# First down phase: where the weight blocks with index 5 and 6 are loaded and when, and chunk 2's output transposes 0.6 later

## The chip, the core and the metric

The kernel runs on one core of one Trainium2 chip. The metric is the device time of one execution in microseconds (us). A core has a matrix engine (PE, with its weight loads shown apart as PEld), a vector engine (DVE), a scalar engine (ACT), a general engine (POOL) and a sequencer for transfers (SP). Transfers between the chip's memory and the on-chip memory are asked for on the queues of SP, POOL and ACT; a queue works through its instructions in their order, so one that waits holds up those behind it.

## The reference

One transformer layer with adaptive layer norm: S = 2048 tokens, width D = 576, 32 heads of 18, a sliding window of 8 keys at distances 0, 2, ..., 14, and a gated feed-forward part of width 4608, without a nonlinearity.

```python
mod = (_silu(c) @ w_mod).reshape(c.shape[0], 6, 1, -1)
sa, ca, ga, sb, cb, gb = ...
h = _layernorm(x) * (1 + ca) + sa
x = x + ga * _A_ref(h, A_wqkv, A_wo)          # windowed attention, then @ wo
h = _layernorm(x) * (1 + cb) + sb
x = x + gb * _B_ref(h, B_w_gate, B_w_up, B_w_down)

def _B_ref(x, w_gate, w_up, w_down):
    h = (x @ w_gate) * (x @ w_up)
    return h @ w_down
```

## The kernel before

The 2048 tokens are cut into 8 chunks of 256. After a prologue (chunk 0's attention and the first steps of chunks 1 and 2) the chunks go through the feed-forward part in five groups, `GROUPS = [[0], [1, 2], [3, 4], [5, 6], [7]]`. For each group there is a gate-up phase (`gate_up`), in which PE makes the 36 tiles `hh[:, f]` of gate times up, and then a down phase (`down`, for the last group `down_last`), in which PE multiplies them by `w_down` into the sums `acc` (columns 0 to 511, line 895) and `accr` (columns 512 to 575, line 900). The attention of later chunks is slipped between these matmuls.

**The down phase of group 0.** One chunk of 256 tokens, so two blocks of 128 rows (`j`); for each of 36 steps `f` there is a pair `mm_a`, `mm_r` for each `j`. Four steps use one block of `w_down` (`FB = 4`, 128 x 4 x 576 bf16, 576 KB), so the phase has 9 blocks, index 0 to 8, and a group's blocks are numbered on from there: 9, 10 and 11 are blocks 0 to 2 of group 1. Steps 0 to 31 run in the loop; block 8 (steps 32 to 35) comes at the end, first all `accr` products, then all `acc` products. Then DVE scales the sums and adds the residual (lines 921 to 930), and the gate-up phase of group 1 follows on PE.

**Where the blocks lie.** `load_wd(g)` (line 171) asks for a block on POOL's queue. It goes to a place of its own if `wd_home` names one, and else to the next of three rotating buffers `wd`. For group 0, blocks 0, 1 and 2 go to the three buffers and blocks 3 and 4 to the half of the `hh` tile that a group of one chunk leaves free; all five are asked for during the gate-up phase. Before the change, block 5 is asked for at the end of block 0, 6 after 1, 7 after 2, then 8 after 5, 9 after 6 and 10 after 7, and 11 at the end of the phase: each goes into the buffer that was just read. `prod_t` holds four products of queries and shifted keys (128 x 1280 bf16 each, line 446) during the attention; groups 1, 2 and 3 already keep two of their blocks in it during their down phases (`ld_prods`, blocks 3 and 4 of the group, asked for at step 32 of the gate-up).

**What lies between the matmuls.** `first_down` lists pieces of later chunks' work in threads. A piece is (PE time, DVE time, marks it needs, its mark, wait until the mark counts, call). `timed` steps through the phase with these estimates, and places a piece behind the step at which its marks are reached, so the order of the instructions is fixed when the kernel is built. In this phase the pieces are: chunk 1's output product and residual (`b_w(1, j)`: lines 588 to 594), its layer norm (`b_ln`, `b_norm`), its transposes by transfer on SP's queue (`b_td`, line 620) and its modulation in place (`b_mod`: lines 294 and 296 on `h2T`); chunk 4's query, key and value products (`a_q`, `a_v`: lines 401, 424, 426), whose values are stored to `vd` on POOL's queue (line 431); and of chunk 2 the weighting of the gathered values (`b_mul`, `b_add`: lines 499 to 509, on the tiles `vsh` that line 440 loads on POOL's queue), then `b_o(2)`, which transposes the attention output `o_sb` on PE (line 517) and copies it to `oT` on ACT (lines 518, 519), then `b_w(2, j)` and its layer norm.

POOL's instructions around the phase are, in order: the loads of `vsh` for chunk 2, a memset of part of `hT` (line 386), the two stores of chunk 4's values, the loads of blocks 5, 6 and 7, then 8, 9, 10 and 11, and the loads of `vsh` for chunk 3.

Of the kernel before, what the change touches and what calls it, by code (L numbers as in the profile page):

```python
# [36 lines left out]
FB = 4  # L37
# [7 lines left out]
def kernel(  # L45
# [45 lines left out]
    def ps(shape, dt, name):  # L91
        return psp.tile(shape, dt, name=name, tag="bank")

    def js(j):
        return slice(j * P, (j + 1) * P)
# [48 lines left out]
    NBLK = FT // FB  # L144

    def load_wgu(g):
        if g >= NG * NBLK:
            return
        cs = slice((g % NBLK) * NB, (g % NBLK + 1) * NB)
        wb = wgu_home.pop(g, None)  # L150
        if wb is None:
            wb = wgup.tile([P, KF, 2, NB], BF, name="wgu")
        for t, wsrc in enumerate((B_w_gate, B_w_up)):
            r = nc.sync.dma_start(wb[:, :, t, :], wsrc[0:KF * P, cs].rearrange("(k p) n -> p k n", p=P))
        wgu_blk[g] = wb
        wgu_in[g] = r
# [6 lines left out]
    def load_wd(g):  # L163
        if g >= NG * NBLK:
            return
        r0 = (g % NBLK) * FB * P
        wb = wd_home.pop(g, None)
        if wb is None:
            wb = wdp.tile([P, FB, D], BF, name="wd")
        wd_blk[g] = wb  # L170
        return nc.gpsimd.dma_start(wb[:], B_w_down[r0:r0 + FB * P, :].rearrange("(k p) n -> p k n", p=P))  # L171
# [239 lines left out]
    def a_q(i, g):  # L411
        qk_tiles(i, QGRP[g], slice(0, CH), nc.scalar.copy)
        if g == 2:
            a_halo(i)
# [4 lines left out]
    def a_v(i, j):  # L419
        hT = aa[i]["hT"]  # L420
        pv = ps([P, VA * DH], F32, "pv")
        pvr = ps([P, VR * DH], F32, "pvr")
        for kt in range(KT):
            nc.tensor.matmul(pv[:], lhsT=hT[:, kt, js(j)], rhs=wv[:, kt, 0:VA * DH], start=(kt == 0), stop=(kt == KT - 1))  # L424
        for kt in range(KT):
            nc.tensor.matmul(pvr[:], lhsT=hT[:, kt, js(j)], rhs=wv[:, kt, VA * DH:D], start=(kt == 0), stop=(kt == KT - 1))
        v_sb = vstage.tile([P, DH, H], BF, name="v_sb")
        nc.scalar.copy(v_sb[:, :, 0:VA], pv[:].rearrange("p (h d) -> p d h", d=DH))
        nc.scalar.copy(v_sb[:, :, VA:H], pvr[:].rearrange("p (h d) -> p d h", d=DH))
        r0 = HALO + i * CH + j * P  # L430
        nc.gpsimd.dma_start(vd[r0:r0 + P, :], v_sb[:].rearrange("p d h -> p (d h)"))
        aa[i].setdefault("v", []).append(v_sb)
# [78 lines left out]
    def b_o(i):  # L511
        pA = ps([P, 4, CH], BF, "oT_pA")
        pB = ps([P, 1, CH], BF, "oT_pB")
        for m in range(KT):
            d = pA[:, m, :] if m < 4 else pB[:, 0, :]
            for j in range(ST):
                nc.tensor.transpose(d[:, js(j)], o_sb[:, j, m * P:(m + 1) * P], ident[:])
        nc.scalar.copy(oT[:, 0:4, :], pA[:])
        nc.scalar.copy(oT[:, 4, :], pB[:, 0, :])
# [64 lines left out]
    def b_w(i, j):  # L584
        pw = ps([P, 512], F32, "pw")
        pwr = ps([P, 64], F32, "pwr")
        for m in range(KT):
            nc.tensor.matmul(pwr[:], lhsT=oT[:, m, js(j)], rhs=wo[:, m, 512:D], start=(m == 0), stop=(m == KT - 1))
        for m in range(KT):
            nc.tensor.matmul(pw[:], lhsT=oT[:, m, js(j)], rhs=wo[:, m, 0:512], start=(m == 0), stop=(m == KT - 1))  # L590
        xt = x1p.tile([P, D], BF, name="x1")
        nc.vector.tensor_tensor(xt[:, 512:D], pwr[:], ga_bc[:, 512:D], ALU.mult)
        nc.vector.tensor_tensor(xt[:, 0:512], pw[:], ga_bc[:, 0:512], ALU.mult)
        nc.vector.tensor_tensor(xt[:], xt[:], x_res[i][:, j, :], ALU.add)
        x1.setdefault(i, []).append(xt)

    def b_ln(i):
        x_res.pop(i)
        bb[i]["xn"], bb[i]["rsq"], bb[i]["norm"] = layernorm(lambda j: x1[i][j], "b", i == 1)
# [238 lines left out]
    def among(n, step, threads):  # L838
        at, (seq, late) = [[] for _ in range(n)], timed([("f", f, step, 0.0, "") for f in range(n)], [], threads, step)
        for kind, x in seq:  # L840
            if kind == "f":
                f = x
            else:
                at[f].append(x)
        return at, late
# [39 lines left out]
    def down(gi, hh, bg):  # L885
        grp = GROUPS[gi]
        nj = ST * len(grp)
        last = FT - FB
        at, late = among(last, 0.25 * nj, bg)
        acc = [ps([P, 512], F32, "acc") for _ in range(nj)]  # L890
        accr = ps([P, 2 * ST, 64], F32, "accr")

        def mm_a(f, j):
            wb = wd_blk[gi * NBLK + f // FB]
            nc.tensor.matmul(acc[j][:], lhsT=hh[:, f, js(j)], rhs=wb[:, f % FB, 0:512],  # L895
                             start=(f == 0), stop=(f == FT - 1))

        def mm_r(f, j):
            wb = wd_blk[gi * NBLK + f // FB]
            nc.tensor.matmul(accr[:, j, :], lhsT=hh[:, f, js(j)], rhs=wb[:, f % FB, 512:D],  # L900
                             start=(f == 0 and j == 0), stop=(f == FT - 1), skip_group_check=True)

        for f in range(last):
            for j in range(nj):
                mm_a(f, j)
                mm_r(f, j)
            if f % FB == FB - 1:
                if f // FB not in (3, 4):
                    load_wd(gi * NBLK + f // FB + (5 if f < 3 * FB else 3))
            asks = (1, 5 * FB, 6 * FB + 2) if gi == 0 else (1, 4 * FB - 1, 6 * FB + 1)  # L910
            if f in asks:
                load_wgu((gi + 1) * NBLK + asks.index(f))
            for piece in at[f]:
                piece()
        xs = [t for i in grp for t in x1.pop(i)]
        for j in range(nj):
            for f in range(last, FT):
                mm_r(f, j)
        o_ts = [outp.tile([P, D], BF, name="o_t") for _ in range(nj)]
        t_r = outr.tile([P, 2 * ST, 64], BF, name="t_r")  # L920
        nc.vector.tensor_tensor(t_r[:, 0:nj, :], accr[:, 0:nj, :],
                                gb_bc[:, None, 512:D].to_broadcast([P, nj, 64]), ALU.mult)
        for j in range(nj):
            for f in range(last, FT):
                mm_a(f, j)
            nc.vector.tensor_tensor(o_ts[j][:, 0:512], acc[j][:], gb_bc[:, 0:512], ALU.mult)
        for j in range(nj):
            r0 = (grp[0] * ST + j) * P
            nc.vector.tensor_tensor(o_ts[j][:, 0:512], o_ts[j][:, 0:512], xs[j][:, 0:512], ALU.add)
            nc.vector.tensor_tensor(o_ts[j][:, 512:D], t_r[:, j, :], xs[j][:, 512:D], ALU.add)  # L930
            nc.sync.dma_start(out_flat[r0:r0 + P, :], o_ts[j][:])
        load_wd(gi * NBLK + NBLK + 2)
        return late
# [260 lines left out]

    def ld_prods(gi):
        for k in range(2):
            g = gi * NBLK + 3 + k
            wd_home[g] = prod_t[:, k * FB * D:(k + 1) * FB * D].rearrange("p (k d) -> p k d", d=D)
            load_wd(g)

# [33 lines left out]
    def first_down(late):  # L1234
        def q(g):
            return (0.53 if g == 2 else 1.07, 0, "h4", "-", 0, lambda: a_q(4, g))

        def v(j):
            return (1.2, 0, "h4", "-", 0, lambda: a_v(4, j))

        def out_1(first):
            return [(0, 0, "", "o1", 1.0, nop), (1.2, 1.35, "o1", "-", 0, lambda: b_w(1, 0)), (1.2, 1.35, "", "x1", 0.5, lambda: b_w(1, 1)),
                    (0, 2.5, "", "s1", 0.7, lambda: b_ln(1)), (0, 0, "s1", "n1", 2.3, lambda: b_norm(1)), (0, 0, "n1", "t1", 9.5, lambda: b_td(1)),
                    (0, 1.0, "t1", "-", 0, lambda: (b_mod(1, (3, 4), False), b_mod(1, (0, 1, 2), True)))]
        a4 = [(0, 0, "", "h4", 1.5, nop)]
        o2 = [(0.55, 0, "o21", "O2", 0.9, lambda: b_o(2)), (1.2, 1.35, "O2", "-", 0, lambda: b_w(2, 0)), (1.2, 1.35, "", "x2", 0.2, lambda: b_w(2, 1)),
              (0, 2.2, "", "s2", 0.7, lambda: b_ln(2)), (0, 1.5, "s2", "n2", 0.2, lambda: b_norm(2)), (0.55, 1.0, "n2", "-", 0, lambda: b_t(2))]
        return [a4, out_1(True), late + [(0, 0, "", "a2", 0.0, nop)] + values_of(2) + o2, [q(0), q(1), q(2), q(3), q(4), v(0), v(1)]]

# [61 lines left out]
```

## Time and profile before

| what | value |
|---|---|
| runs (median of 3; lowest, highest) | 552.38 us; 551.4, 554.15 |
| profiled execution: its own time, span | 551.74 us, 550.0 us |
| PE busy | 538.7 us, 98% of the span |
| DVE, ACT, POOL busy | 318.2, 250.1, 70.4 us |
| granted PE clock | 0.999 |
| moved by transfers | 114.52 MB, mean 208 GB/s |
| gate-up of group 0 | 57 to 100.7 us |
| down phase of group 0 | 100.7 to 134.8 us |
| gate-up of group 1 | 134.8 to 213 us |

Durations are those of one profiled execution; 1.74 us of its own time lie outside the span. PE's matmuls are pipelined: one `acc` and one `accr` product together start every 0.245 us, though their durations in the trace are 0.38 and 0.19 us. A row of the timeline gives the start, the duration, the engine, the line, the operation and tiles, how many instructions are merged, and in brackets how long the engine sat idle before it and what ended that.

### The profile page before, as it was taken

How to read it: one execution, taken by the hardware profiler on the slowest of the kernel's cores; microseconds unless marked ns; L12 is line 12 of the kernel's file. 1: busy time of each engine (PE TensorE's matmuls, PEld its weight loads, DVE VectorE, ACT ScalarE, POOL GpSimd, SP SyncE). 2: the span in 40 equal slices, each digit the busy share in tenths (PEclk: the TensorE clock that was granted, in tenths of full speed). 3: DMA queues.
4: the chain of work that ended last, by engine and by line, in shares of the span. 5: the costliest groups of instructions: out<-in, count | busy, mean ns of one | idle time of the engine just before them, and what ended most of it. 6: DMA issues, size and time to landing. Idle time of an engine off the chain costs nothing.

```text
span 550.0 us, 14590 instructions
## 1 busy us (share of the span) xinstructions
PE 538.7 (98%) x6190; PEld 322.1 (59%) x6190; DVE 318.2 (58%) x717; ACT 250.1 (45%) x615; POOL 70.4 (13%) x106
## 2 busy tenths in 40 slices
PE   8999999989999999999999999999999999999997
PEld 4777799745845544555544444555544444558875
DVE  5989587765867688555438895544333934032212
ACT  3666777640756554021655553012655551006630
POOL 8112111023000110102000200111030001020030
PEclk9999999999999999999999999999999999999999
DMA  8999989569883583767835790986289531849871
GB/s 286 299 299 354 305 221 301 204 192 271 293 228 124 190 214 137 167 188 230 308 104 163 186 326 20 181 229 189 77 213 307 166 89 44 263 130 269 278 231 52
DMA packets 94746, 114.52 MB, mean 208 GB/s; under 512 B 27930, under 2 KB 83370, under 8 KB 94554
## 3 DMA queue, kind: packets, MB, share of 16 engines
q1 hardware_dynamic: 83184, 67.29, 43.0%
q0 software_dynamic: 11344, 46.25, 26.8%
q8 instruction: 48, 0.79, 0.6%
q14 instruction: 16, 0.13, 0.1%
q10 hardware_dynamic: 154, 0.07, 0.0%
HBM read 103.15 MB, written 4.74 MB: 196 GB/s over the span
## 4 chain that ended last, share of the span: by engine, by line
PE 80%; issue 7%; DMA 6%; DVE 5%; ACT 1%; POOL 0%; SPq 0%; POOLq 0%; DVEq 0%; ACTq 0%
PE pg L694 26%; PE pu L694 21%; PE acc L895 14%; DMA wd<-in_B_w_down_dram 4%; PE pq L694 3%; PE acc L947 3%; DMA wgu<-in_B_w_up_dram 2%; PE accr L900 2%; PE pq L401 2%; PE lgT L455 2%; PE pv L694 2%; PE pw L590 2%; DVE prod_t L1032 1%; PE pv L424 1%; PE busy L190 1%
## 5 line engine op out<-in xcount | busy, mean ns | idle before, releaser
L694 PE MATMUL pg<-h2T,wgu 64*128 64x512 bf16 (+1 forms) x1472 | 277.2, 327 | 0.0
L694 PE MATMUL pu<-h2T,wgu 64*128 64x512 bf16 (+1 forms) x1472 | 275.4, 327 | 0.5 <-DMA wgu<-in_B_w_up_dram 0.5
L694 PEld LDWEIGHTS <-wgu 64*128 64x128 bf16 x2944 | 144.9, 94 | 97.0 <-DMA wgu<-in_B_w_up_dram 1.0
L745 ACT CAST u_sb<-pu 128x512 bf16<-128x512 f32 (+1 forms) x172 | 85.5, 497 | 142.3 <-PE pg L694 135.3
L748 DVE TENSOR_TENSOR hh<-g_sb,u_sb 128x512 bf16<-128x512 bf16 x136 | 57.4, 424 | 117.2 <-ACT g_sb L746 116.6
L895 PE MATMUL acc<-wd,hh 128*128 128x512 bf16 x392 | 97.4, 380 | 2.0 <-DMA wd<-in_B_w_down_dram 2.0
L746 ACT CAST g_sb<-pg 128x512 bf16<-128x512 f32 (+1 forms) x172 | 86.6, 503 | 0.0
L895 PEld LDWEIGHTS <-hh 128*128 128x128 bf16 x504 | 49.0, 98 | 59.7 <-issue 1.5
L900 PE MATMUL accr<-wd,hh 128*128 128x64 bf16 x392 | 66.7, 193 | 1.0 <-DMA wd<-in_B_w_down_dram 1.0
L694 PE MATMUL pu<-h2T,wgr 64*128 64x512 bf16 (+1 forms) x188 | 61.5, 327 | 0.2 <-ACT u_sb L745 0.2
L694 PE MATMUL pg<-h2T,wgr 64*128 64x512 bf16 (+1 forms) x188 | 61.5, 327 | 0.0
L171 POOL DMA_DIRECT2D wd<-in_B_w_down_dram x33 | 24.8, 753 | 229.6 <-PE accr L900 96.0
L900 PEld LDWEIGHTS <-hh 128*128 128x128 bf16 x504 | 45.9, 98 | 5.3 <-issue 3.4
L446 DVE TENSOR_TENSOR prod_t<-qT,kT 128x1280 bf16<-128x1280 bf16 x56 | 43.7, 819 | 0.7 <-ACT kT L765 0.7
L499 DVE TENSOR_TENSOR vsh<-vsh,attn 128x1152 bf16<-128x1152 bf16 x56 | 39.7, 750 | 0.0
L694 PEld LDWEIGHTS <-wgr 64*128 64x128 bf16 x376 | 19.0, 94 | 15.4 <-issue 2.5
L440 POOL DMA_DIRECT2D vsh<-vd x14 | 12.6, 899 | 105.5 <-DVE o_sb L509 79.2
L895 PE MATMUL acc<-prod_t,hh 128*128 128x512 bf16 x96 | 24.5, 380 | 0.0
L296 ACT ACTIVATE h2T<-h2T,modc 128x256 bf16<-128x256 bf16 x12 | 6.6, 594 | 37.5 <-DMA h2T<-xn 37.5
L401 PE MATMUL pq<-hT,wqk 128*128 128x256 bf16 (+1 forms) x225 | 21.8, 251 | 0.5 <-DVE hT L294 0.5
L694 PE MATMUL pq<-hT,wqk 64*128 64x256 bf16 (+1 forms) x360 | 21.7, 259 | 0.0
L506 DVE TENSOR_TENSOR vsh<-vsh 128x1152 bf16<-128x1152 bf16 x28 | 20.2, 752 | 0.0
(201 smaller groups left out, 562.8 us busy)
## 6 DMA issues: line engine op xcount, KB each, us to landing
wgu<-in_B_w_gate_dram SPq DMA_DIRECT2D x44, 512.0 KB, 4.2
wgu<-in_B_w_up_dram SPq DMA_DIRECT2D x44, 512.0 KB, 7.1
wd<-in_B_w_down_dram POOLq DMA_DIRECT2D x33, 576.0 KB, 5.3
vsh<-vd POOLq DMA_DIRECT2D x14, 1152.0 KB, 9.9
hh<-in_B_w_down_dram POOLq DMA_DIRECT2D x6, 576.0 KB, 7.6
prod_t<-in_B_w_down_dram POOLq DMA_DIRECT2D x6, 576.0 KB, 10.9
x_r<-in_A_x_dram SPq DMA_DIRECT2D x8, 288.0 KB, 11.3
vd<-v_sb POOLq DMA_DIRECT2D x16, 144.0 KB, 4.7
```

The lines of the kernel that those rows point to most:

```text
L171: return nc.gpsimd.dma_start(wb[:], B_w_down[r0:r0 + FB * P, :].rearrange("(k p) n -> p k n", p=P))
L401: nc.tensor.matmul(pq[:, gi, :], lhsT=wqk[:, kt, m * P:(m + 1) * P], rhs=hT[:, kt, cols], start=(kt == 0), stop=(kt == KT - 1))
L446: nc.vector.tensor_tensor(prod, aa[i]["qT"][:], aa[i]["kT"][:, :, off:off + CH], ALU.mult)
L499: nc.vector.tensor_tensor(v, v, at, ALU.mult)
L506: nc.vector.tensor_tensor(vsh[:, d], vsh[:, d], vsh[:, 4 + 2 * s:6 + 2 * s], ALU.add)
L694: return nc.tensor.matmul(out, lhsT=lhs, rhs=rhs, start=first, stop=last, skip_group_check=True)
L745: nc.scalar.copy(u[:, c, :], pu)
L746: nc.scalar.copy(g[:, c, :], pg)
L748: return lambda: nc.vector.tensor_tensor(hh[:, f - c:f + 1, :], g, u, ALU.mult)
L895: nc.tensor.matmul(acc[j][:], lhsT=hh[:, f, js(j)], rhs=wb[:, f % FB, 0:512], start=(f == 0), stop=(f == FT - 1))
L900: nc.tensor.matmul(accr[:, j, :], lhsT=hh[:, f, js(j)], rhs=wb[:, f % FB, 512:D], start=(f == 0 and j == 0), stop=(f == FT - 1), skip_grou ...
L947: nc.tensor.matmul(acc[i][:], lhsT=hh[:, f, js(j)], rhs=wb(f)[:, c0:c1], start=(f == 0), stop=(f == FT - 1))
```

## The change

Three edits, all for the down phase of group 0.

First, blocks 5 and 6 of group 0 get places in `prod_t`, by a call of `ld_prods(0)` in the first piece of the phase (the piece `h4`, which held an empty call before). Second, the requests behind the loop's blocks follow a table: for group 0 the end of block 0 asks for block 7, of 1 for 8, of 2 for 9 and of 7 for 10; the other groups keep what they had. Third, the thread of chunk 2 gets an empty piece `z2` with a wait of 0.6 us by the planner's clock ahead of `b_o(2)`.

```diff
             if f % FB == FB - 1:
-                if f // FB not in (3, 4):
-                    load_wd(gi * NBLK + f // FB + (5 if f < 3 * FB else 3))
+                ask = {0: 7, 1: 8, 2: 9, 7: 10} if gi == 0 else {0: 5, 1: 6, 2: 7, 5: 8, 6: 9, 7: 10}
+                if f // FB in ask:
+                    load_wd(gi * NBLK + ask[f // FB])
...
     def ld_prods(gi):
         for k in range(2):
-            g = gi * NBLK + 3 + k
+            g = gi * NBLK + (5 if gi == 0 else 3) + k
             wd_home[g] = prod_t[:, k * FB * D:(k + 1) * FB * D].rearrange("p (k d) -> p k d", d=D)
             load_wd(g)
...
-        a4 = [(0, 0, "", "h4", 1.5, nop)]
-        o2 = [(0.55, 0, "o21", "O2", 0.9, lambda: b_o(2)), ...
+        a4 = [(0, 0, "", "h4", 1.5, lambda: ld_prods(0))]
+        o2 = [(0, 0, "o21", "z2", 0.6, nop), (0.55, 0, "z2", "O2", 0.9, lambda: b_o(2)), ...
```

In the order of the built program, the two loads stand on POOL's queue right behind the memset of `hT` and ahead of the two stores of chunk 4's values; behind the stores come blocks 7, 8, 9, 10 and 11. On PE, `b_o(2)` stands two steps later (four pairs of `acc` and `accr`), `b_w(2, 0)` three steps later and `b_w(2, 1)` one step later than before. On DVE, the three modulations of chunk 1's `h2T` now stand ahead of the residual of `b_w(2, 0)` instead of behind it. The orders on ACT and SP are the same.

More of the change, by code (lines that the diff above doesn't have):

```diff
@@ L1244, in out_1 @@
                     (0, 1.0, "t1", "-", 0, lambda: (b_mod(1, (3, 4), False), b_mod(1, (0, 1, 2), True)))]
-        a4 = [(0, 0, "", "h4", 1.5, nop)]
-        o2 = [(0.55, 0, "o21", "O2", 0.9, lambda: b_o(2)), (1.2, 1.35, "O2", "-", 0, lambda: b_w(2, 0)), (1.2, 1.35, "", "x2", 0.2, lambda: b_w(2, 1)),
+        a4 = [(0, 0, "", "h4", 1.5, lambda: ld_prods(0))]
+        o2 = [(0, 0, "o21", "z2", 0.6, nop), (0.55, 0, "z2", "O2", 0.9, lambda: b_o(2)), (1.2, 1.35, "O2", "-", 0, lambda: b_w(2, 0)), (1.2, 1.35, "", "x2", 0.2, lambda: b_w(2, 1)),
               (0, 2.2, "", "s2", 0.7, lambda: b_ln(2)), (0, 1.5, "s2", "n2", 0.2, lambda: b_norm(2)), (0.55, 1.0, "n2", "-", 0, lambda: b_t(2))]
```

## The prediction

> **What bounds the kernel now.** I read the page first (PE is busy 538.7 of 550.0 us, granted clock 0.999), then cut the span into its phases, then asked what PE waits for, then followed POOL's queue and PE's weight loads through the down phase of group 0. The windows by phase (gate-up of group 0, its down phase, gate-up of group 1):
>
> ```profile
> core 0: us, PE busy (x) PEld busy (x) DVE busy (x) ACT busy (x) POOL busy (x), PEclk, DMA share, GB/s
> ...
> 57.00:100.70 43.70, 43.52 (x780) 38.65 (x776) 31.11 (x63) 34.87 (x107) 5.45 (x8) 1.00 0.98 286
> 100.70:134.80 34.10, 31.15 (x262) 17.96 (x259) 22.92 (x50) 10.62 (x26) 5.62 (x8) 1.00 0.66 206
> 134.80:213.00 78.20, 78.20 (x987) 45.07 (x988) 59.36 (x124) 46.58 (x112) 6.94 (x9) 1.00 0.73 216
> ```
>
> PE is without a gap in the phase behind (78.20 of 78.20) and lacks 2.95 us in the middle one (34.10 less 31.15). So PE sets the time, and what is taken out of this phase comes out of the end, unless a later phase waits for something that does not move with PE. The waits of PE:
>
> ```profile
> PE acc L895 <- DMA wd<-in_B_w_down_dram: 2.0, 1, 2.0
> ...
> PE accr L900 <- DMA wd<-in_B_w_down_dram: 1.0, 2, 0.6
> ...
> PE oT_pA L517 <- DVE o_sb L509: 0.3, 1, 0.3
> ```
>
> All of the first, the longer one (0.6) of the second and the third fall in this phase: 2.05 + 0.60 + 0.30 = 2.95 us. Why a block of `w_down` is late, the timeline of POOL shows:
>
> ```profile
> 98.17 0.31 POOL L386 MEMSET hT<- 64x256 bf16 x1 [1.75 <-PE pu L694]
> 111.89 0.55 POOL L431 DMA_DIRECT2D vd<-v_sb  x1 [13.41 <-ACT ln_rstdb L267]
> 115.41 0.54 POOL L431 DMA_DIRECT2D vd<-v_sb  x1 [2.96 <-ACT v_sb L429]
> 115.95 2.26 POOL L171 DMA_DIRECT2D wd<-in_B_w_down_dram  x3
> 127.30 0.76 POOL L171 DMA_DIRECT2D wd<-in_B_w_down_dram  x1 [9.10 <-PE accr L900]
> ```
>
> Blocks 5, 6 and 7 stand behind two stores of chunk 4's values, which wait for ACT until 115.41, though the buffers of blocks 0 to 2 were read earlier. Block 5 is asked for at 115.95 and lands at 123.62 (the chain of waits gives 7.67 us). Block 8 can be asked for only when block 5 has been read, at 127.30, and lands at 132.71 (5.41). The timeline of the weight loads measures the three gaps by starts:
>
> ```profile
> 120.93 0.51 PEld L517 LDWEIGHTS <-o_sb 128*128 128x128 bf16 x9 [0.45 <-DVE o_sb L509]
> ...
> 123.66 0.10 PEld L900 LDWEIGHTS <-hh 128*128 128x128 bf16 x1 [2.17 <-issue]
> ...
> 132.75 0.27 PEld L900 LDWEIGHTS <-hh 128*128 128x128 bf16 x7 [0.70 <-issue]
> ```
>
> That is 0.45 + 2.17 + 0.70 = 3.32 us. The PE rows give 2.95 because they end a gap's start with the modelled end of a matmul (0.38 us long, though the next pair starts 0.245 us behind). I take 3.32, since the next start is what a removed wait brings forward, and 2.95 as its lower bound.
>
> **Blocks 5 and 6, early.** The two loads follow the memset of `hT` on POOL, so they are issued at 98.48 and 99.23 (0.75 us each, from 2.26 for three). Their space is free: the last reader of `prod_t`, a product of line 455, starts at 76.0. The slowest load of line 171 took 14.5 us, so both are there by 113.8. Block 5 is wanted at 120.41, where its steps now begin ahead of the transposes. The store that POOL does next waits until 111.89 anyway, so nothing on its queue is pushed back. The wait of 2.17 us goes.
>
> **Blocks 7, 8 and 9.** They take the three places at 115.95, 116.70 and 117.46 that 5, 6 and 7 had, beside the same four requests for gate and up weights on SP's queue: the same bytes in the same seconds. I put PE's new order on the clock, 0.245 us a pair. At 120.41 come four pairs, at 121.39 ten transposes (their starts are 0.057 apart), at 121.96 six pairs, at 123.43 `b_w(2, 0)` (1.22, from 124.64 to 125.86), four pairs, at 125.63 `b_w(2, 1)`, at 126.85 ten pairs; block 7 is wanted at 127.34, block 8 at 129.30. The first of the old three landed at 123.62; the second was wanted at 126.84 without a wait, so it was there. Block 7 has 3.7 us in hand and block 8 at least 2.4. With the slowest `wd` load of the trace (10.3) block 8 would land at 127.0. The wait of 0.70 goes. Blocks 9 and 10 are wanted a phase later; 11 stays where it is.
>
> **The transposes.** At 121.39 they stand 0.51 us behind the end of `o_sb` (120.42 + 0.46), so 0.45 goes. ACT's copies to `oT` ended at 122.83, 1.90 behind the transposes' restart at 120.93, or 1.96 behind a gapless start: 123.35 now. `b_w(2, 0)` at 123.43 has 0.08 to spare; the row is one case, so I bound this term by 0 and 0.2 of new wait, and take 0.
>
> **DVE.** It had 4.11 us without work before line 592 at 124.98. The three modulations (0.92 us in all) move into it. They wait for the transposes by transfer, issued on SP from 113.47 to 116.0, landing after at most 3.4: 119.4, so they start at 120.9, and `b_w(2, 0)`, in line behind them, finds DVE free at 121.8. The layer norm of `b_w(2, 1)` ends 4.51 us behind its start (127.82 to 132.33), so at 130.14. The scaling of `accr` would be ready at 129.73 and waits 0.41; but the next thing, `acc`, came 0.87 behind `accr`'s scaling before, with 0.57 of it idle, so it is hidden. Chunk 2's normalization on ACT stands behind the next phase's first casts (137.07), 4.7 us after its input before and 3.6 now: hidden.
>
> The sum is 551.74 - 3.32 = 548.4 us, measured against the profiled execution's own time (span 550.0 and 1.74 outside it); against the median of the runs, 552.38, it would be 549.1. By the lower bound and 0.2 of new wait it is 549.0. Half a per cent is 2.76 us, about what a measurement of this kernel can tell from no change.
>
> **Rival 1: the moved transfers delay chunk 2's values.** The two `vsh` loads at 93.52 and 95.52 landed after 8.4 and 10.4 us, by order 101.92 and 105.9, and DVE uses the first at 102.21 with 0.29 to spare. Moving 1.18 MB to 98.5 puts it beside them, in 5 us windows that already moved 346 and 310 GB/s; the window behind, 105 to 110, moved 2. If both share evenly from 99.2 on, the first lands up to 2.7 later; with all 1.18 MB ahead of it at 350 GB/s, 3.4. DVE would then free the accumulators of `b_w(1, 0)` later; it ended that at 104.38, and PE's next product in need of one starts at 105.81, so 1.43 is free. The loss is 1.3 to 2.0, and the time 549.7 to 550.4. For it: the thin 0.29. Against: `vsh` and `wd` are issued on one queue (q0 of the page), `vsh` first, and DVE idles 2.34 at 112.06, which absorbs the rest of its delay. [...] I give this rival 0.12.
>
> **Rival 2, slower than before.** It is the same place, with the values held long. Beyond 3.32 + 1.43 = 4.75 us of delay (landing at 106.7, which is 13.2 after the issue) the loss outgrows the gain. The slowest `vsh` load of the trace took 13.4, and the slowest load of any on POOL 14.5: at the latter the delay is 6.1, the loss 4.7, and the time 553.1. For over half a per cent the delay must pass 7.5. Against it: 1.18 MB is 3.4 us of transfer at the rates seen. I give it 0.04.
>
> **Rival 3: a block is still late.** If the burst at 116 is slower than read here, block 8 would have to land behind 129.30; at the 132.71 of before 3.4 would be lost again and nothing gained, at 131 1.7, so 550.1. The four weight requests on SP speak for it; that the third place served block 7 without a wait at 130.0 speaks against. I give it 0.06.
>
> **Rival 4: the time comes back later.** Group 1's gate-up begins 3.3 us sooner, and if its weights or chunk 2's `h2T` were fixed in time, PE would wait there: 551.7, no change. But its first weights were asked for at 91.95, the next two at 116.06, and what follows is asked for behind PE's own reads. I give it 0.06.
>
> **How the numbers follow.** The forecast case has 0.72. Within it I put 0.86 on more than 2.76 us (the bounds 2.75 and 3.32 lie at and above that, and runs of before differ by 2.75), so 0.62; with a little from rivals 1 and 3, faster is 0.64. Slower is 0.03 (rival 2 mostly stays within the half per cent). The rest, 0.33, is same. The likeliest time is 548.4. The range goes from 547.0 (the lowest run, 551.4, less 3.32, and 1.1 for what the profiled execution may have had less of) to 551.0, which takes in the lower bound, rival 1, the half of rival 3, and 0.6 of scatter.
>
> **What would show it.** Right: POOL's two loads onto `prod_t` at about 98.5 and 99.2; no wait of line 895 or 900 for `wd` before the phase's end, which comes at 131.4 to 131.5 instead of 134.8; no wait for `o_sb` at line 517; the span near 546.7. Wrong: DVE's line 499 waiting for `vsh` behind 102.2 and PE's line 401 waiting for DVE (rivals 1 and 2); line 900 still waiting for `wd` (3); a phase that is shorter by 3.3 with a span that is not (4); or line 588 waiting for ACT by more than 0.2.

## The result and the profile after

The changed kernel takes 549.12 us (median of 20 runs, 548.06 to 553.42) beside 552.91 us for the kernel before (20 runs, 551.23 to 556.15). The ratio is 0.9934, with a 95% interval of 0.9918 to 0.995: faster by 0.66%, some 3.7 us (the interval is 2.8 to 4.5 us). The profiled execution took 549.95 us, with a span of 548.2. It gave back part of what the first down phase gained, as shown below.

The windows of the changed kernel, cut where its first down phase ends:

```profile
core 0: us, PE busy (x) PEld busy (x) DVE busy (x) ACT busy (x) POOL busy (x), PEclk, DMA share, GB/s
...
57.00:100.70 43.70, 43.51 (x780) 38.69 (x776) 31.10 (x63) 34.88 (x107) 6.94 (x10) 1.00 1.00 287
100.70:131.40 30.70, 30.70 (x264) 17.90 (x263) 22.63 (x50) 10.59 (x26) 4.11 (x6) 1.00 0.71 227
```

PE has no gap left in the phase (30.70 of 30.70). The timeline of POOL says why: the two loads into `prod_t` go out ahead of the stores, and the three behind the stores are now blocks 7, 8 and 9.

```profile
98.15 0.31 POOL L386 MEMSET hT<- 64x256 bf16 x1 [1.25 <-PE pu L694]
98.66 1.51 POOL L171 DMA_DIRECT2D prod_t<-in_B_w_down_dram  x2 [0.20 <-issue]
111.86 0.56 POOL L431 DMA_DIRECT2D vd<-v_sb  x1 [11.69 <-ACT ln_rstdb L267]
115.38 0.56 POOL L431 DMA_DIRECT2D vd<-v_sb  x1 [2.96 <-ACT v_sb L429]
115.93 2.25 POOL L171 DMA_DIRECT2D wd<-in_B_w_down_dram  x3
```

The timeline of PE, with the transposes, the two output products and the first matmul of the next phase; no row has a bracket, so none waited:

```profile
121.36 0.61 PE L517 MATMUL oT_pA<-shifts,o_sb 128*128 128x128 bf16 x8
...
123.39 0.31 PE L588 MATMUL pwr<-wo,oT 128*128 128x64 bf16 x5
...
125.60 0.31 PE L588 MATMUL pwr<-wo,oT 128*128 128x64 bf16 x5
...
131.33 0.28 PE L694 MATMUL pg<-h2T,wgr 64*128 64x256 bf16 x1
```

The next phase starts at 131.33 instead of 134.81: 3.48 us sooner. But the span is only 1.8 shorter. The waits of PE in this execution name the rest:

```profile
PE pu L694 <- DMA wgu<-in_B_w_up_dram: 1.6, 2, 0.8
...
PE accr L900 <- DMA wd<-in_B_w_down_dram: 0.4, 1, 0.4
```

Both of the first kind lie in the last group's gate-up, some 370 us later. The timeline of the weight loads there:

```profile
501.93 0.77 PEld L694 LDWEIGHTS <-wgu 64*128 64x128 bf16 x15 [1.02 <-DMA wgu<-in_B_w_up_dram]
...
514.73 0.77 PEld L694 LDWEIGHTS <-wgu 64*128 64x128 bf16 x15 [1.12 <-DMA wgu<-in_B_w_up_dram]
```

Together they are 2.1 us. Whether the change causes them is settled below.

### The profile page after: what moved, and what is told of

Its sections match the earlier page's. It is cut to its first block, busy times and chain, and to the rows that moved or that the text cites. A ratio compares the mean times of both kernels' runs of the same rounds, so it can differ in the third digit from the quotient of the medians.

```text
span 548.2 us, 14589 instructions
## 1 busy us (share of the span) xinstructions
PE 538.7 (98%) x6190; PEld 322.5 (59%) x6190; DVE 317.6 (58%) x717; ACT 250.0 (46%) x615; POOL 70.2 (13%) x106
## 4 chain that ended last, share of the span: by engine, by line
PE 83%; DMA 7%; DVE 4%; issue 4%; ACT 1%; SPq 0%; POOL 0%; POOLq 0%; DVEq 0%; ACTq 0%
PE pg L694 25%; PE pu L694 20%; PE acc L895 16%; DMA wgu<-in_B_w_up_dram 5%; PE pq L694 3%; PE pq L401 3%; PE acc L948 3%; PE pw L590 2%; PE accr L900 2%; PE lgT L455 2%; PE pv L694 2%; DMA wd<-in_B_w_down_dram 1%; PE pv L424 1%; DVE prod_t L1033 1%; PE busy L190 1%
## 5 line engine op out<-in xcount | busy, mean ns | idle before, releaser
L694 PEld LDWEIGHTS <-wgu 64*128 64x128 bf16 x2944 | 147.3, 94 | 98.4 <-DMA wgu<-in_B_w_up_dram 2.8
L895 PE MATMUL acc<-wd,hh 128*128 128x512 bf16 x376 | 93.2, 380 | 0.0
L900 PE MATMUL accr<-wd,hh 128*128 128x64 bf16 x376 | 63.5, 193 | 0.4 <-DMA wd<-in_B_w_down_dram 0.4
L171 POOL DMA_DIRECT2D wd<-in_B_w_down_dram x31 | 23.3, 751 | 227.9 <-PE pwr L588 95.6
L694 PEld LDWEIGHTS <-wgr 64*128 64x128 bf16 x376 | 21.1, 94 | 15.4 <-issue 2.5
L895 PE MATMUL acc<-prod_t,hh 128*128 128x512 bf16 x112 | 28.9, 380 | 0.0
L900 PE MATMUL accr<-prod_t,hh 128*128 128x64 bf16 x112 | 21.6, 193 | 0.0
```

Source lines behind the costliest of these rows:

```text
L694: return nc.tensor.matmul(out, lhsT=lhs, rhs=rhs, start=first, stop=last, skip_group_check=True)
```

## The experiments

**The loads without the shift.**

```diff
-        o2 = [(0, 0, "o21", "z2", 0.6, nop), (0.55, 0, "z2", "O2", 0.9, lambda: b_o(2)), ...
+        o2 = [(0.55, 0, "o21", "O2", 0.9, lambda: b_o(2)), ...
```

> The first two edits without the 0.6 of z2, so the transposes of chunk 2 stand where they stood before. My theory (three waits of PE, each with its own cause): the waits for blocks 5 and 8 (2.17 + 0.70) go; the wait for o_sb (0.45) stays, and the output product, now only four pairs behind the transposes, waits for ACT's copies (oT ready at 122.8, wanted at 122.4: 0.45 new). The phase is 2.4 shorter than before and ends at 132.4, against 131.33 with all three edits. Rival (the transfers alone carry it, the 0.6 is decoration): the phase ends within 0.2 of 131.33.

The weight loads of PE in this kernel:

```profile
120.89 0.51 PEld L517 LDWEIGHTS <-o_sb 128*128 128x128 bf16 x9 [0.45 <-DVE o_sb L509]
122.56 0.37 PEld L588 LDWEIGHTS <-oT 128*128 128x128 bf16 x5 [0.32 <-ACT oT L518]
132.14 0.10 PEld L694 LDWEIGHTS <-wgr 64*128 64x128 bf16 x2 [0.42 <-issue]
```

Both waits that the theory names are there, 0.45 for `o_sb` and 0.32 for ACT's copies (0.45 was expected). The phase ends at 132.14 and not within 0.2 of 131.33, so the rival falls. (The 0.42 in the last row stands ahead of the next phase's first weight load in the kernel before too, with or without a wait of PE.) The loads give 2.67 of the 3.48 us, the shift 0.81 on top of them. The ratio to before is 0.9943 (0.9924 to 0.9962), which overlaps that of the changed kernel: the 0.81 is read from the profiles, and the times of the whole kernel do not show it.

**The shift without the loads.** The kernel before, with the `z2` piece alone:

```diff
-        o2 = [(0.55, 0, "o21", "O2", 0.9, lambda: b_o(2)), ...
+        o2 = [(0, 0, "o21", "z2", 0.6, nop), (0.55, 0, "z2", "O2", 0.9, lambda: b_o(2)), ...
```

> The third edit alone, loads as before. My theory: block 5 still lands at about 123.6 and its steps are now wanted at 120.4, so the wait for it grows to 3.2 and swallows the wait for o_sb; everything behind it follows without a stop, block 8 is asked for at 126.2 and lands at 131.6, before it is wanted at 132.5. The phase ends at 134.6, 0.2 earlier than before: the shift is worth next to nothing without the loads. Rival (the shift is what shortens the phase): an end at or before 133.9, 0.9 earlier.

Neither came in the profiled execution: the phase ended at 136.28, 1.5 later than before, and the ratio is 1.0018 (0.9995 to 1.004). The wait itself is as expected:

```profile
123.68 0.10 PEld L900 LDWEIGHTS <-hh 128*128 128x128 bf16 x1 [3.23 <-issue]
```

What was not expected stands in the windows behind it, in the column after the engines, the granted clock:

```profile
120.00:123.70 3.70, 0.56 (x7) 0.24 (x4) 1.58 (x5) 0.00 (x0) 0.00 (x0) 1.00 1.02 362
123.70:128.20 4.50, 4.50 (x29) 2.65 (x29) 0.00 (x0) 2.27 (x4) 0.05 (x1) 0.62 1.07 348
```

After 3.23 us with nothing to do the clock averages 0.62 over the next 4.5 us. From about 124.65 to 128.07 a pair of `acc` and `accr` takes 0.48 us instead of 0.245; 3.4 us at half pace cost 1.7, which is the distance from the expected 134.6 to 136.28. The slow stretch thus began 0.97 us behind the end of the standstill and lasted 3.42 us; from 128.20 to 136.30 the clock was 1.00 again. Why it fell, and why for that long, is not shown.

The profiled execution is not the common one. Its granted clock over the whole span is 0.997; of the 12 executions of this kernel 4 have 0.994 to 0.997, and the other 8 have 0.999 or 1.000. So the clock falls in some executions and not in others, and the ratio leaves open whether the shift alone costs anything.

**The same wait, filled with useless work.** To tell the clock from other causes of the slow stretch, twelve matmuls were placed in the wait:

```diff
         for f in range(last):
+            if gi == 0 and f == 5 * FB:
+                fill = ps([P, 512], F32, "fill")
+                for _ in range(12):
+                    nc.tensor.matmul(fill[:], lhsT=hh[:, 0, js(0)], rhs=hh[:, 0:2, :], start=True, stop=True)
             for j in range(nj):
```

> The kernel with the shift alone, and twelve matmuls of 512 columns whose result is not used, placed on PE ahead of block 5's first matmul, where PE waited 3.2 us for the load; at the pace of a 512-column matmul (some 0.22 each) they last 2.6 us. My theory (in the run with the shift alone the long standstill made the clock fall to 0.62 for the next 4.5 us): PE now works through most of the wait, the clock stays at 1.00 and the phase ends at 134.6 instead of 136.28, though PE does more. Rival (the slow stretch behind the wait comes from the loads or from ACT): the slow pace stays and the phase ends at 136.3 or later.

The windows of the same two stretches:

```profile
120.00:123.70 3.70, 3.17 (x19) 1.35 (x17) 1.62 (x5) 0.00 (x0) 0.00 (x0) 1.00 1.03 366
123.70:128.20 4.50, 4.50 (x43) 2.60 (x43) 0.29 (x2) 2.27 (x4) 0.75 (x1) 1.00 1.07 348
```

Block 5 came at the same time (123.70), PE stood for 0.81 instead of 3.23, the clock stayed at 1.00, 43 matmuls fit where 29 had, and the phase ended at 134.78. The ratio to before is 0.9982 (0.9967 to 0.9998), below that of the shift alone by 0.36%, though the two intervals just overlap. In none of its 12 executions is the clock over the whole span below 0.999. So the slow stretch follows the standstill, and not the loads or ACT, which are the same in both; one profile of each and 4 of 12 against 0 of 12 would be thin by themselves, and the counts of all the kernels, given further down, bear it out.

**The same places, asked for late.** The changed kernel, with `ld_prods(0)` called at the end of block 0:

```diff
+                if gi == 0 and f == FB - 1:
+                    ld_prods(0)
                 if f // FB in ask:
                     load_wd(gi * NBLK + ask[f // FB])
...
-        a4 = [(0, 0, "", "h4", 1.5, lambda: ld_prods(0))]
+        a4 = [(0, 0, "", "h4", 1.5, nop)]
```

> All three edits, but the two loads into the product space are asked for at the end of block 0, so they stand on POOL's queue behind the two stores of chunk 4's values, at 115.9. Same space, same order of the loads. My theory (the queue holds the loads up, not the lack of a place): block 5 lands at about 123.6 as before, PE waits about 3.2 for it at 120.4, and the phase ends at about 134.6. Rival (the places bring the gain, since blocks 7 and 8 no longer wait for buffers): the phase ends at 132.0 or before.

```profile
122.58 0.10 PEld L900 LDWEIGHTS <-hh 128*128 128x128 bf16 x1 [2.13 <-issue]
...
133.84 0.10 PEld L694 LDWEIGHTS <-wgr 64*128 64x128 bf16 x2 [0.42 <-issue]
```

The wait for block 5 is back, but it is 2.13 us and not 3.2, as the block landed 1.0 sooner than in the two kernels before; why is open. The phase ends at 133.84, between the two theories, 0.97 sooner than before. The ratio is 1.0002 (0.9981 to 1.0024): with the same places and the same order of loads, the later request leaves nothing of the gain that can be measured. The free places do remove the wait for block 8; a wait of 0.26 us for block 6, at 125.43, is new.

**The stores on another queue.** The kernel before, with chunk 4's two stores on SP:

```diff
-        nc.gpsimd.dma_start(vd[r0:r0 + P, :], v_sb[:].rearrange("p d h -> p (d h)"))
+        (nc.sync if i == 4 else nc.gpsimd).dma_start(vd[r0:r0 + P, :], v_sb[:].rearrange("p d h -> p (d h)"))
```

> The kernel before, with the two stores of chunk 4's values on SP's queue instead of POOL's; no load moves to the product space, nothing else changes. My theory (the queue): block 5 is asked for when block 0 has been read, at 112.6, and lands before 119; its wait of 2.17 goes, the wait for o_sb of 0.45 stays, a new wait of up to 0.45 for ACT's copies comes, and block 8, asked for at 124.6, lands at about 130 when it is wanted. The phase ends at about 132.4. Rival (blocks 5 to 7 are late because buffers are freed late): the phase stays within 0.3 of 134.8.

POOL's timeline shows that the queue was what held block 5:

```profile
113.02 0.77 POOL L171 DMA_DIRECT2D wd<-in_B_w_down_dram  x1 [14.55 <-PE accr L900]
```

It is asked for as soon as block 0 has been read, and PE does not wait for it. But the phase ended at 136.53 and the ratio is 1.0027 (1.0008 to 1.0047), which neither theory gave. The stores now hold up SP's queue:

```profile
111.60 3.86 SPq L431 DMA_DIRECT2D vd<-v_sb  x2
115.56 2.64 SPq L620 DMA_TRANSPOSE h2T<-xn  x2
118.25 0.63 SPq L154 DMA_DIRECT2D wgu<-in_B_w_gate_dram  x1
```

The transposes go out 2.1 later than before (113.47) and the requests for gate and up weights 2.2 later (116.06). Blocks 7 and 8 then come late, and the clock falls again:

```profile
129.19 0.10 PEld L900 LDWEIGHTS <-hh 128*128 128x128 bf16 x1 [0.97 <-issue]
133.28 0.27 PEld L900 LDWEIGHTS <-hh 128*128 128x128 bf16 x7 [2.07 <-issue]
```

```profile
133.30:137.00 3.70, 3.70 (x22) 1.45 (x23) 1.34 (x3) 0.00 (x0) 0.10 (x1) 0.60 1.05 351
```

The transposes by transfer took 9.9 us to land instead of 3.0, and from 120 to 125 us the transfers moved 118 GB/s instead of 363. That the later requests on SP's queue are what made the blocks late is argued from this, not shown. The clock is the smaller part of the loss: the 9 of the 12 executions whose clock over the whole span stayed at 0.999 or above have a median of 554.03, all 12 one of 554.32.

**Where the profile's 1.7 us went.** The kernel before and the changed kernel once more, both unaltered.

> The kernel before once more, for a second profile. My theory for the 1.7 us that the changed kernel's profile gave back behind the down phase (ahead by 3.5 at 250 us, by 1.8 at the end): a scatter of the waits for gate and up weights in the last group's gate-up, which any execution of any of these kernels can have; the first profile of before happened to have none there. So a second profile of before may show 0 to 2 us of such waits behind 486 us. Rival (the earlier down phase causes them): none here, as in the first profile.

> The changed kernel once more. Scatter theory: the end of the first down phase is again within 0.1 of 131.33 and 3.5 ahead; the waits for gate and up weights behind 486 us come out differently from the first 1.6, anywhere from 0 to 2; the ratio to before is 0.992 to 0.995. Rival (the change causes the waits): again two waits of about 0.8 at the same places.

The kernel before has the same waits as the first time: 0.44, 2.17 and 0.69 in the phase, which ended at 134.77, and a span of 550.0 us. The changed kernel's phase ended at 131.44. Its span is 546.3 us, 3.7 below before; the ratio is 0.9942 (0.9917 to 0.9967). The list of PE's waits, which goes by modelled ends, names no wait for gate and up weights behind 486 us in either profile. The rows of the weight loads, by which the first profile's waits are 2.1 us, show one short wait in each, first in the kernel before, then in the changed one:

```profile
524.35 0.76 PEld L694 LDWEIGHTS <-wgu 64*128 64x128 bf16 x15 [0.39 <-DMA wgu<-in_B_w_up_dram]
```

```profile
516.74 0.77 PEld L694 LDWEIGHTS <-wgu 64*128 64x128 bf16 x15 [0.32 <-DMA wgu<-in_B_w_up_dram]
```

So the kernel before can have such a wait too, which its rival theory denied, and the two waits of the first profile did not come again. A third profile came with the next comparison:

> The changed kernel for comparison. Theory: the first down phase ends within 0.15 of 131.33 again, with no wait for a block of it; the waits behind 486 us come out anywhere from 0 to 2; a ratio of 0.992 to 0.995 to before.

The phase ended at 131.34, with one wait of 0.82 us behind 486 us (0.5 by modelled ends), and the ratio is 0.9934 (0.9913 to 0.9956). By the weight loads PE thus waited 2.1, 0.3 and 0.8 us for gate and up weights in the last group in three profiles of the changed kernel, 0 and 0.4 in two of before, and 2.3 and 1.0 in those of the shift alone and of the stores on SP, whose phases ended later than before's. The waits come and go with the same program, and an earlier down phase is not needed for them. What decides them is open.

**A fourth buffer in the last group.** Those waits have a remedy of their own:

```diff
+        if gi == NG - 1:
+            wgu_home[gi * NBLK + 3] = spare[gi][:, 0:8 * NB].rearrange("p (k t n) -> p k t n", t=2, n=NB)
+            load_wgu(gi * NBLK + 3)
...
-                    ask = {1: 4, 2: 5, 3: 6, 5: 7, 6: 8}.get(f // FB, NBLK) if gi == 0 else f // FB + 2
+                    ask = {1: 4, 2: 5, 3: 6, 5: 7, 6: 8}.get(f // FB, NBLK) if gi == 0 else f // FB + (3 if gi == NG - 1 else 2)
```

> The changed kernel, and in the last group block 3 of the gate and up weights goes into the half of the hh tile that a group of one chunk leaves free, so that each block behind it is asked for four steps earlier. My theory (a block is asked for only when one of three buffers has been read, so its latency scatter shows): the waits behind 486 us go, and the time falls by 0.5 to 1.5 against the changed kernel, a ratio of 0.990 to 0.993 to before. Rival (the transfers' rate is the limit there): waits of 1 to 2 us stay and the time is that of the changed kernel.

> The kernel with the fourth buffer in the last group once more, beside the changed kernel on the same chip. Theory: no wait for gate and up weights behind 486 us in a second profile either, and a median 0.5 to 1.5 below the changed kernel's. Rival (the absence of waits was one lucky execution): waits of 0.5 to 2 us there, and medians within 0.4.

In neither profile does PE wait for gate and up weights behind 486 us; the spans are 546.2 and 546.8. The medians are 548.03 and 548.27, beside 549.17 and 548.73 of the changed kernel on the same chips: 1.1 and 0.5 us lower. The ratios to before are 0.992 (0.9894 to 0.9946) and 0.9925 (0.9907 to 0.9943). Their intervals overlap those of the changed kernel, so that this version beats it is likely and not shown. That the buffer removes the waits is not shown either: the first profile of before and that of the filled kernel have none there without it.

## Why the prediction was right

**The sum.** The three gaps by starts made 3.32 us; the phase became shorter by 3.48, 3.33 and 3.43 us in three profiles (131.33, 131.44 and 131.34, the first beside 134.81 and the others beside 134.77). Reading the gaps by starts rather than by the modelled ends (2.95) was the right choice. The forecast of 548.4 started from the profiled execution; the alternative from the median of three runs, 549.1, is what the 20 runs gave, but in part by luck: the median of before over 20 runs is 552.91, from which the sum gives 549.6. The whole kernel gained some 3.7 us, and its interval of 2.8 to 4.5 us does not tell that from 3.32. The step that missed a little is the span near 546.7: 548.2 in the first profile, 546.3 and 547.5 later, in good part by the waits in the last group.

**Blocks 5 and 6.** They were issued at 98.66 and the following 0.75, against 98.48, and landed 9.5 and 10.0 after. **Blocks 7 and 8** were in time: the slowest load into `wd` in the phase took 10.2 us, so block 8, asked for at about 116.7, was there by 126.9 and was wanted at 129.3. **The transposes and DVE** went as worked out. ACT's copies ended at 123.30 (forecast 123.35), 0.09 ahead of the output product at 123.39 (forecast 0.08). DVE's rows:

```profile
102.19 1.42 DVE L499 TENSOR_TENSOR vsh<-vsh,attn 128x1152 bf16<-128x1152 bf16 x2
...
120.39 0.46 DVE L509 TENSOR_TENSOR o_sb<-vsh 128x576 bf16<-128x576 bf16 x1
120.76 0.85 DVE L294 TENSOR_SCALAR h2T<-h2T,modc 128x256 bf16<-128x256 bf16 x3
...
130.02 0.24 DVE L922 TENSOR_TENSOR t_r<-accr,gb_bc 128x128 bf16<-128x128 f32 x1
130.57 0.69 DVE L927 TENSOR_TENSOR o_t<-acc,gb_bc 128x512 bf16<-128x512 f32 x1 [0.31 <-PE acc L895]
```

The modulations filled the idle time at 120.8, and the scaling of `accr`, forecast to be held to 130.14 and hidden, came at 130.02 with 0.31 to spare.

**Rivals 1 and 2** are answered by the first of these rows: line 499 took chunk 2's values at 102.19 (102.21 before) without a wait. The landing of the two `vsh` loads is

```profile
DMA to landing us min/median/max: 8.0/9.1/10.1
```

against 8.4 and 10.4 before, while the loads behind them on the same queue took 9.5 and 10.0. They were asked for at 94.0 and 96.0, 0.5 later than before, so the first landed at about 102.0 and the spare time was 0.2. In this execution, then, the 1.18 MB behind them on the queue did not make the two loads of `vsh` slower than before; how the transfers of one queue are served is not shown beyond that. **Rival 3** (a block is still late) did not come. **Rival 4** (the time comes back later) seemed to have come in the first profile, and the repeats showed that the change is not needed for it.

**What the prediction did not see** is the clock. At 2.17 us the old wait left it at 1.00 in both profiles of before, but over the whole span the granted clock was 0.996 or 0.997 in 14 of 67 executions of the kernel before, timed beside the experiments, and in 1 of 37 of the changed kernel. The other kernels part in the same way. Those whose profile has a standstill of PE of more than 2 us in this phase show a clock of 0.994 to 0.997 in 4 of 12 (shift alone), 5 of 12 (asked late) and 3 of 12 executions (stores on SP), with before 26 of 103. Those without show it in 0 of 11 (loads without the shift), 0 of 12 (filled) and 0 of 12 (fourth buffer), with the changed kernel 1 of 72.

In three comparisons before's executions at the lower clock had medians of 553.59 (6), 553.37 (3) and 552.91 (5), the others 551.88 (28), 551.79 (9) and 552.59 (16). So some of the 3.7 us may come from such executions; an estimate from 14 of 67 and the 1.7 us of the shift alone is 0.35 us in the mean. That it was the old wait that slowed PE in them is inferred from the counts and the run with the shift alone: no profile of before caught one.

## What to carry to other kernels

A load that seems to wait for a buffer may wait for its queue: look at what stands ahead of it, and give it a free place and a request ahead of the store that blocks, since moving the store to another queue moved the blockage with it (what stood behind it on SP's queue went out 2.1 us later). When a wait is removed, look for the next one a few steps on; the shift of two steps was worth 0.81 us in the profiles with the loads, and nothing that could be measured without them. Measure a gap by the starts on both sides, and take a second profile before a difference far from the change is explained by the change.

## What the runs showed of the hardware

In the profiled execution with the shift alone a standstill of PE of 3.23 us cost a further 1.7 us, as the granted clock fell (0.62 over the next 4.5 us); filling it with useless matmuls kept the clock at 1.00 and ended the phase 1.5 us sooner than with the wait. In the run with the stores on SP a standstill of 2.07 us, which began 2.0 us after the end of one of 0.97 us, was followed by a clock of 0.60 over the next 3.7 us. In both profiles of the kernel before a standstill of 2.17 us, which began 0.6 us after the end of one of 0.45 us (0.44 in the second), was followed by 1.00, with a pair of `acc` and `accr` every 0.245 us.

So the length alone does not decide, and the same kernel goes both ways: with the shift alone the clock over the whole span was lower in 4 of 12 executions, in the kernel before in 14 of 67. How long the standstill was in the executions without a profile is not shown. What decides whether the clock falls is not shown either.
